# Attention and gated feed-forward in one kernel: a new order of the attention cycle, other cycles for the weight-narrowing jobs, all bias loads on one queue

## The chip, the cores and the metric

The kernel runs on one core of a Trainium2 chip. The metric is the device time of one execution in microseconds (us). Engines are named as in the profile: PE (TensorE, matrix products and transposes), DVE (VectorE), ACT (ScalarE), POOL (GpSimd) and SP (SyncE, which only issues DMAs here). L12 is line 12 of the kernel before.

## What is computed

Attention over 4 batches, 8 heads, 576 positions and head size 64, with a bias made from positions, and on its output a feed-forward block with a convolution of three taps and a gate, all in float32:

```python
scores = scale * np.matmul(q, k.transpose(0, 1, 3, 2))
...
bias = h @ w2
scores = scores + bias.transpose(2, 0, 1)[None, :, :, :]
...
attn = np.exp(scores)
attn = attn / (np.sum(attn, axis=-1, keepdims=True) + 1e-09)
return np.matmul(attn, v).astype(np.float32)
...
h = np.maximum(x @ w_in, 0.0)
...
gate = 1.0 / (1.0 + np.exp(-conv_out))
return (h * gate @ w_out).astype(np.float32)
```

## The kernel before, in words

The program has three stretches. First it makes the bias table (up to about 80 us). Then it works through 16 head pairs n = (p, b): pair p of heads, batch b, with b running fastest. Last comes the feed-forward block (from about 285 us), which keeps PE busy without a gap and which the change does not touch.

The attention stretch is a software pipeline, written out by hand as a list CYCLE (L888). Cycle m runs the entries for pair n = m and the first ones for pair m+1. An entry such as `S:3,1,0:P` has a name, a unit t (0 to 4, a block of query rows), a head h, an offset to m, and the engine. The program issues each engine's instructions in the order of the list, and an engine takes its instructions strictly in that order. The entries:

- S (scores, L438): products of queries and keys on PE into one of four pairs of PSUM banks. R (reduce, L471): DVE adds the bias tile and takes the row maximum. E (expo, L487): ACT exponentiates and sums rows.
- T and s (L531): PE transposes the exponentials. k0, k1, k0b, k1b and c copy them from PSUM to SBUF, on ACT or DVE by the letter at the end.
- P (L570): PE multiplies by the values, in groups 0 and 1 of five parts; xb copies the result out. P:0 is the last PE work of a cycle.
- ia, inv, sm, rt, st, sp: the row sums, inverted on DVE, turned on PE, copied, stored to DRAM and read back over all partitions into `rb`, of which there is one. AN (L638, L995): POOL multiplies the output of pair m-3 by rb.
- X (L229): for most pairs queries and keys are split for exact products into a high and a low part by POOL, in three pieces of two instructions each. `is_split(n)` is true for n = 3, 4, 6, 7, 8, 10, 11, 12 and 14, so X stands in cycles m = 2, 3, 5, 6, 7, 9, 10, 11 and 13. The first scores of pair m+1 need all three pieces.
- J1, J2, J3 and W (L875): the 28 jobs that narrow a piece of the feed-forward weights to float32 and split it. J1 is an integer shift on DVE (L161), J2 one ACT instruction, J3 an integer combination on DVE (L166), W two POOL instructions (L194, L195). J2 also issues the load for the third job after it. `per_pair` (L854) says how many jobs a cycle has; the unit of an entry (0, 2, 4) picks the first, second and third.

The three tiles that S, R, E and T of a unit share are used in turn, and a matrix product that takes a pair of banks waits for the copies or reductions out of it. Bias tiles for the next pair of heads are loaded in the cycles m = 3, 7 and 11 (b = 3), each as soon as its last reduction is issued; tiles 0 to 2 on SP's queue, 3 and 4 on POOL's (L248). `load(n + 2)` brings queries and keys after the last scores of pair n.

AN waits for the newest first shift of an earlier cycle:

```python
mul = apply_norm(n)
if shifts:
    tc.add_manual_dep(mul.ins, shifts.pop(max(shifts)).ins.name, DATA)
```

Of the kernel before, what the change touches and what calls it, by code (L numbers as in the profile page):

```python
# [13 lines left out]
ALU = mybir.AluOpType  # L14
# [4 lines left out]
def attention_ffn_kernel(  # L19
# [11 lines left out]
    nc = tc.nc  # L31
    B, S, DM = out.shape
# [5 lines left out]
    P = 128  # L38
# [159 lines left out]
    with tc.manual_schedule():  # L198
# [29 lines left out]

        def split_qk(n, k):  # L229
            x, lo, hi, cs = qks[n], qk_t[1][n % 2], his[(n + 1) % 2], chunks[k]  # L230
            nc.gpsimd.tensor_scalar(hi[:, cs], x[:, cs], 1.0, 0.0, op0=ALU.mult, op1=ALU.add)  # L231
            nc.gpsimd.tensor_sub(lo[:, cs], x[:, cs], hi[:, cs].bitcast(F32))  # L232

        vz_p = pool(att, "vz", 1)
# [11 lines left out]
            nc.sync.dma_start(vt[TL:P, 9], v[b, p, TL:P, 4])  # L246

        def load_bias(p, t, cuts=()):  # L248
            queue = nc.gpsimd if p and t not in (0, 1, 2) else nc.sync
            bt = bias_p.tile([P, 2, S], F32, name="bt") if t else bias0_p.tile([P, 1, S], F32, name="bt0")  # L250
            for a, e in zip((0,) + cuts, cuts + (P,)):
                for h in range(2):
                    c = (2 * p + h) * BW
                    if t:
                        i0 = TL + (t - 1) * P
                        queue.dma_start(bt[a:e, h], bias_rows[i0 + a:i0 + e, c:c + S])
                    else:
                        queue.dma_start(bt[TL * h:TL * h + TL, 0, :], bias_rows[0:TL, c:c + S])
            biast[p, t] = bt
# [21 lines left out]
        inv = bias_c.tile([P, 4 * NBLK], F32, name="inv")  # L281
# [114 lines left out]
        xb = {0: x0}  # L396
# [3 lines left out]
        DATA = mybir.DependencyInfo(mybir.DependencyClass.Sync, mybir.DependencyReason.DATA)  # L400
# [15 lines left out]
        def turned_sp(n, t):  # L416
            spt[n, t] = (sps[1][spt[n, t][1]], None)
# [317 lines left out]
        first = [(0, 0), (0, 1), (0, 2), (0, 3)]  # L735
# [4 lines left out]
        def heads(t):  # L740
            return (0, 1) if t else (0,)
# [109 lines left out]
                fill.extend(pv_parts(n, t > 2))  # L851

        NJ = 4 * KC + 2 * FE
        per_pair = [0, 0, 2, 2, 3, 2, 2, 1, 3, 2, 2, 1, 3, 2, 2, 1]  # L854
        first_job = {sum(per_pair[0:n]): n for n in range(NSEQ) if per_pair[n]}

        def job_slices(j):
            if j < 4 * KC:
                return w_in[j // 4 * P:j // 4 * P + P], wi[j // 4], slice(j % 4 * 256, j % 4 * 256 + 256)
            f = (j - 4 * KC) // 2  # L860
            return w_out[f * P:f * P + P], wo[f], slice(j % 2 * 256, j % 2 * 256 + 256)
# [8 lines left out]
        held = []  # L870
        now, used, drawn_at = [None], [0], [0]
        side_in = {}
        left, shifts = {}, {}

        def job_step(j, k):  # L875
            if k == 1:
                _, dst, cs = job_slices(j)
                jobs[j] = split_w_steps(e_p, dst[:, :, cs], raw_w.pop(j), ("cv", "cv"))
            ins = next(jobs[j])
            if k == 1 and j in first_job:  # L880
                shifts[first_job[j]] = ins
# [6 lines left out]
        CYCLE = """  # L888
            E:1,1,0:A X:0,1:G E:1,0,0:A S:2,0,0:P R:2,0,0:V S:2,1,0:P S:3,0,0:P X:1,1:G S:3,1,0:P ia:-1:A
            X:2,1:G R:2,1,0:V E:2,0,0:A s:1,0:P T:0,0:P k0:0,0:A P:1,0,-1:P R:3,1,0:V P:1,1,-1:P k1:0,0:A  # L890
            E:2,1,0:A P:1,2,-1:P R:3,0,0:V P:1,3,-1:P inv:-2:V E:3,1,0:A P:1,4,-1:P k1b:0,0:A k0b:0,0:V T:1,0:P
            AN:-3:G xb:1,-1:V inv:-1:V S:4,0,0:P S:4,1,0:P E:3,0,0:A J1:0,0:V k1:1,0:A s:2,0:P c:1,0:V k0:1,0:A
            T:2,0:P R:4,0,0:V R:4,1,0:V T:3,0:P J2:0,0:A S:0,0,1:P c:2,0:V k1:2,0:V E:4,0,0:A S:1,0,1:P k0:2,0:A
            J1:2,0:V E:4,1,0:A R:0,0,1:V S:1,1,1:P k1:3,0:A k0:3,0:V sm:-1:P J3:0,0:V s:4,0:P W:0,0:G J2:2,0:A
            sp:-2:G s:3,0:P T:4,0:P J3:2,0:V P:0,0,0:P P:0,1,0:P rt:-1:A R:1,1,1:V k1:4,0:V W:2,0:G J1:4,0:V
            J2:4,0:A J3:4,0:V W:4,0:G k0:4,0:A P:0,2,0:P R:1,0,1:V E:0,0,1:A P:0,3,0:P st:-1:G c:4,0:A P:0,4,0:P
            c:3,0:A xb:0,0:V
        """.split()

        begun = {(k, t, h, 2) for k, t, h in (  # L900
# [18 lines left out]
        def emit(op, copy):  # L919
            k, n = op[0], op[-1]  # L920
            t = op[1]
            if k == "S":
                scores(n, t, op[2])
                now[0] = pair[n, t, op[2]]
                used[0], drawn_at[0] = 0, len(clock)
                slots[now[0]][2] = -1 - len(clock)
                if (t, op[2]) == (4, 1) and n + 2 < NSEQ:
                    load(n + 2)
                    for later, x in held:
                        later(x)  # L930
                    held.clear()
            elif k == "R":
                reduce(n, t, op[2])
                left[n, t] = left.get((n, t), len(heads(t))) - 1
                p, b = seq[n]
                if not left[n, t] and b == B - 1 and p + 1 < NP:
                    load_bias(p + 1, t)
            elif k == "E":
                expo(n, t, op[2])
            elif k == "s":  # L940
                turned_sp(n, t) if spt[n, t][1] is not None else None
                side_of[n, t] = side_cols((n, t))
                side_transposes(side_of[n, t], n, t)
            elif k == "T":
                turned_sp(n, t) if spt[n, t][1] is not None else None
                turned[n, t] = transposes(n, t)
                after_turn(n, t)
            elif k in ("k0", "k1", "k0b", "k1b"):
                d, c = place(n, t, int(k[1]) if t else 0)
                v = turned[n, t][int(k[1])]  # L950
                done(turned_in[n, t])
                if t:
                    copy(d[:, 0:8, c:c + TL], v)
                elif k == "k0":
                    copy(d[:, 0:4, 0:TL], v[:, 0:4])
                elif k == "k0b":
                    copy(d[0:TL, 4, 0:TL], v[0:TL, 4])
                elif k == "k1":
                    copy(d[:, 5:9, 0:TL], v[:, 1:5])
                else:  # L960
                    copy(d[TL:P, 4, 0:TL], v[TL:P, 0])
            elif k == "c":
                d, c = place(n, t, 0)
                copy(halves(d[:, 8, c:c + P]), side_of.pop((n, t)))
                done(side_in.pop((n, t)))
            elif k == "P":
                g, c = op[1], op[2]
                if c == 0:
                    parts_of[n, g] = pv_parts(n, g, False)
                parts_of[n, g][c]()  # L970
                if (g, c) == (1, 4) and n + 2 < NSEQ:
                    if seq[n][1] == B - 1 and ("S", 4, 1, n + 1) not in begun:
                        held.append((load_v, n + 2))
                    else:
                        load_v(n + 2)
            elif k == "xb":
                pv_out(n, op[1], copy)
            elif k == "X":
                if is_split(n):
                    split_qk(n, t)  # L980
            elif k == "ia":
                add_eps(n)
            elif k == "inv":
                invert(n)
            elif k == "sm":
                sum_in[n] = side_cols(n)
                sum_transposes(sum_in[n], n)
            elif k == "rt":
                copy_sums(n, sum_in.pop(n), copy)
                done(side_in.pop(n))  # L990
# [38 lines left out]
        for m in range(1, NSEQ + 1):  # L1029
# [4 lines left out]
            for entry in CYCLE:  # L1034
                k, at, eng = entry.split(":")
# [117 lines left out]
        for b in range(B):  # L1153
# [28 lines left out]
            for c in range(KC):  # L1182
# [4 lines left out]
                lambda f, gi, t=t: gs[b, f][:, gi, t * P:(t + 1) * P] for t in range(NT)  # L1187
# [98 lines left out]
```

## Time and profile before

| | us |
|---|---|
| median of 3 runs (lowest to highest) | 481.1 (478.8 to 484.03) |
| the profiled execution | 480.15 |
| its span, first to last instruction | 478.3 |
| PE busy in the span | 458.1 |
| DVE, ACT, POOL busy | 350.9, 314.4, 162.9 |

The span is 1.85 us shorter than the execution's own time. The profile gives the busy time of each engine, what each waited for, and for any stretch a timeline. A PE that is shown busy can still have waited inside a group of instructions, so the length of a cycle, from one P:0 to the next, tells more than the idle time alone.

### The profile page before, as it was taken

What the parts mean: (1) busy time and instruction counts of PE and PEld (TensorE: products, weight loads), DVE (VectorE), ACT (ScalarE), POOL (GpSimd) and SP (SyncE); (2) the same over time, 40 slices, a digit from 0 to 9 for tenths busy, and PEclk for the clock granted to TensorE, in tenths of its full rate; (3) what the DMA queues carried; (4) which work ended last, traced back from release to release, by engine and by line L of the source; (5) the groups of instructions that cost most, each with busy time, mean ns of one, the idle gap of its engine ahead of it and who ended that gap; (6) DMA issues with size and microseconds to landing.
All of it is one profiled execution on the core that took longest, in us unless ns stands there. A gap on an engine that the chain in (4) does not pass through costs nothing.

```text
span 478.3 us, 10920 instructions
## 1 busy us (share of the span) xinstructions
PE 458.1 (96%) x4095; PEld 342.1 (72%) x4095; DVE 350.9 (73%) x818; ACT 314.4 (66%) x769; POOL 162.9 (34%) x194
## 2 busy tenths in 40 slices
PE   5988899999999999999999999999999999999996
PEld 3333356777677777777577768988888888888886
DVE  6999967788888788888888612893499149936971
ACT  6999876898888979988789722871364126414530
POOL 1000001493777837874667427006000500060000
PEclk9999999999999999999999999999999999999999
DMA  1899857688868977699861300001000200020003
GB/s 39 228 346 305 315 191 176 188 244 210 201 171 188 259 202 187 148 261 230 199 175 54 114 25 26 2 0 66 24 0 1 88 22 1 1 89 1 0 4 107
DMA packets 33768, 60.81 MB, mean 127 GB/s; under 512 B 6300, under 2 KB 15028, under 8 KB 33716
## 3 DMA queue, kind: packets, MB, share of 16 engines
q1 hardware_dynamic: 32372, 56.24, 41.8%
q0 software_dynamic: 960, 3.54, 2.8%
q8 instruction: 32, 0.52, 0.5%
q10 hardware_dynamic: 384, 0.35, 0.2%
q14 instruction: 20, 0.16, 0.1%
HBM read 44.12 MB, written 15.98 MB: 126 GB/s over the span
## 4 chain that ended last, share of the span: by engine, by line
PE 74%; DMA 11%; DVE 8%; issue 3%; ACT 2%; POOL 1%; SPq 0%; DVEq 0%
PE bank L108 35%; PE pair L108 31%; PE bank L111 7%; DMA bt<-bias_d 4%; DMA bias_d<-st 3%; DVE sp L476 2%; DVE y L325 2%; DVE ptx L155 1%; DMA vt<-in_v_dram 1%; ACT y L321 1%; DMA raw_w<-in_moe_w_in_dram 1%; ACT st L368 1%; DMA qk<-in_qk_dram 1%; DMA pars<-in_par_dram 1%; DVE pty L155 1%
## 5 line engine op out<-in xcount | busy, mean ns | idle before, releaser
L476 DVE CUSTOM_DVE_ANT_0 sp<-pair,bt 128x576 f32<-128x576 f32 x144 | 104.7, 751 | 17.8 <-PE pair L108 7.6
L490 ACT ACTIVATE sp<-sp,nm 128x576 f32<-128x576 f32 x144 | 111.2, 776 | 9.9 <-DVE nm L476 9.4
L108 PE MATMUL pair<-xs,wi 128*128 128x512 f32 x384 | 88.9, 391 | 0.0
L108 PE MATMUL bank<-wo,g 128*128 128x512 f32 x384 | 87.7, 389 | 0.0
L108 PEld LDWEIGHTS pair<-xs,wi 128*128 128x128 f32 x384 | 71.7, 188 | 15.7 <-issue 0.9
L108 PEld LDWEIGHTS bank<-wo,g 128*128 128x128 f32 x384 | 72.0, 188 | 14.9
L111 PE MATMUL bank<-identr,sr 64*128 64x64 f32 x1184 | 60.5, 245 | 5.1 <-DVE nm L476 3.0
L111 PEld LDWEIGHTS bank<-identr,sr 64*128 64x128 f32 x1184 | 53.8, 136 | 14.6 <-issue 5.8
L1071 DVE SCALAR_TENSOR_TENSOR cv<-h,cw,cv 128x575 f32<-128x575 f32 x64 | 52.3, 818 | 12.6 <-ACT cv L1066 10.6
L690 ACT ACTIVATE h<-pair 128x512 f32<-128x512 f32 x32 | 19.1, 597 | 55.5 <-PE pair L108 54.4
L231 POOL TENSOR_SCALAR hi<-qk 128x640 fp32r<-128x640 f32 (+1 forms) x27 | 19.2, 711 | 83.6 <-DMA qk<-in_qk_dram 79.4
L325 DVE TENSOR_SCALAR y<-tl,inv,nb 128x576 f32<-128x576 f32 (+33 forms) x112 | 47.6, 501 | 0.0
L194 POOL TENSOR_SCALAR xs<-x 128x512 fp32r<-128x512 f32 (+1 forms) x16 | 11.3, 704 | 105.4 <-DVE gt L1091 105.3
L108 PE MATMUL bank<-ptx,vt 128*64 128x320 f32 x320 | 47.0, 438 | 0.0
L108 PE MATMUL pair<-qk 64*128 64x288 f32 (+1 forms) x280 | 40.6, 433 | 4.0 <-DVE nm L476 2.7
L108 PE MATMUL pair<-y,pars 128*32 128x512 f32 (+8 forms) x352 | 42.3, 499 | 1.8 <-DVE y L325 1.0
L232 POOL TENSOR_TENSOR ql<-qk,hi 128x640 fp32r<-128x640 f32 (+1 forms) x27 | 41.0, 1517 | 2.3
L152 ACT ACTIVATE ptx<-bank 128x256 f32<-128x256 f32 (+2 forms) x92 | 39.1, 460 | 1.5 <-PE bank L111 0.8
L108 PE MATMUL bank<-pty,vt 128*64 128x256 f32 x320 | 38.1, 384 | 0.0
L1077 ACT ACTIVATE cv<-cv 128x576 f32<-128x576 f32 x32 | 21.9, 683 | 22.0 <-DVE cv L1071 21.9
L1078 DVE SCALAR_TENSOR_TENSOR cv<-cv,h 128x576 f32<-128x576 f32 x32 | 24.1, 752 | 14.0 <-ACT cv L1077 14.0
L108 PEld LDWEIGHTS pair<-y,pars 128*32 128x32 f32 x352 | 15.1, 112 | 26.4 <-DVE y L325 11.8
(90 smaller groups left out, 702.0 us busy)
## 6 DMA issues: line engine op xcount, KB each, us to landing
qk<-in_qk_dram SPq DMA_DIRECT2D x32, 320.0 KB
bias_d<-st SPq DMA_DIRECT2D x13, 607.0 KB
bt<-bias_d SPq DMA_DIRECT2D x18, 288.0 KB
qk<-in_qk_dram SPq DMA_DIRECT2D x32, 144.0 KB
rb<-r_d SPq DMA_DIRECT2D x32, 144.0 KB
vt<-in_v_dram SPq DMA_DIRECT2D x16, 256.0 KB
raw_w<-in_moe_w_in_dram SPq DMA_DIRECT2D x16, 256.0 KB
out_dram<-o SPq DMA_DIRECT2D x16, 256.0 KB
```

Source lines behind the costliest of these rows:

```text
L108: return use(nc.tensor.matmul(o, *args, **kw), o)
L111: return use(nc.tensor.transpose(o, *args), o)
L152: return noted(nc.scalar.activation(o, i, AF.Copy), i)
L231: nc.gpsimd.tensor_scalar(hi[:, cs], x[:, cs], 1.0, 0.0, op0=ALU.mult, op1=ALU.add)
L232: nc.gpsimd.tensor_sub(lo[:, cs], x[:, cs], hi[:, cs].bitcast(F32))
L325: nc.vector.tensor_scalar(y, dist[:, 0:n], inv[:, ig:ig + 1], nb1, op0=ALU.mult, op1=ALU.max)
L476: use(nc.vector.tensor_tensor_reduce(out=halves(spt[n, t][0][:, h]), in0=ps[:, :, 0:HS], in1=halves(bt[:, h]), op0=ALU.add, op1=ALU.min, s ...
L490: exps[n, t, h] = nc.scalar.activation(sp[:, h], sp[:, h], AF.Exp, bias=nm[:, h:h + 1], scale=-1.0, accum_out=sms[n][:, col:col + 1],)
L690: use(nc.scalar.activation(h[:, 0:NM], ps[:, 0], AF.Relu), ps)
L1071: nc.vector.scalar_tensor_tensor(out=cv[:, o:o + S - 1], in0=h[:, i:i + S - 1], scalar=cw[:, f, kk:kk + 1], in1=cv[:, o:o + S - 1], op0=AL ...
L1077: nc.scalar.activation(cv, cv, AF.Tanh, scale=0.5)
L1078: nc.vector.scalar_tensor_tensor(out=cv, in0=cv, scalar=1.0, in1=h, op0=ALU.add, op1=ALU.mult)
```

## The change

Six edits: the third piece of X waits for the newest J1 issued so far; AN waits for the newest J1 issued so far, and no longer for the newest first one; all bias tiles go to SP's queue; `per_pair` is new, with three jobs only in cycles without X and none or one where bias tiles are loaded; a cycle with fewer than three jobs leaves out the first places, not the last; and CYCLE is in a new order (its first line stands here).

```diff
-            nc.gpsimd.tensor_scalar(hi[:, cs], x[:, cs], 1.0, 0.0, op0=ALU.mult, op1=ALU.add)
+            first = nc.gpsimd.tensor_scalar(hi[:, cs], x[:, cs], 1.0, 0.0, op0=ALU.mult, op1=ALU.add)
+            if k == 2 and shifts:
+                tc.add_manual_dep(first.ins, shifts[-1].ins.name, DATA)
...
-            queue = nc.gpsimd if p and t not in (0, 1, 2) else nc.sync
+            queue = nc.gpsimd if p and t not in (0, 1, 2, 3, 4) else nc.sync
...
-        per_pair = [0, 0, 2, 2, 3, 2, 2, 1, 3, 2, 2, 1, 3, 2, 2, 1]
+        per_pair = [0, 0, 2, 1, 3, 2, 2, 0, 3, 2, 2, 0, 3, 2, 3, 3]
...
-        left, shifts = {}, {}
+        left, shifts = {}, []
...
-            if k == 1 and j in first_job:
-                shifts[first_job[j]] = ins
+            if k == 1:
+                shifts.append(ins)
...
-            E:1,1,0:A X:0,1:G E:1,0,0:A S:2,0,0:P R:2,0,0:V S:2,1,0:P S:3,0,0:P X:1,1:G S:3,1,0:P ia:-1:A
+            S:2,0,0:P E:1,0,0:A ia:-1:A inv:-1:V E:1,1,0:A T:0,0:P S:2,1,0:P S:3,0,0:P R:2,0,0:V J1:0,0:V
...
-                    tc.add_manual_dep(mul.ins, shifts.pop(max(shifts)).ins.name, DATA)
+                    tc.add_manual_dep(mul.ins, shifts[-1].ins.name, DATA)
...
-                if t // 2 < per_pair[n]:
-                    job_step(sum(per_pair[2:n]) + t // 2, 4 if k == "W" else int(k[1]))
+                job = t // 2 - (3 - per_pair[n])
+                if job >= 0:
+                    job_step(sum(per_pair[2:n]) + job, 4 if k == "W" else int(k[1]))
```

The instructions themselves stay as they are; lines after L232 move down by two or three. Three places in the order of the instructions follow.

PE in cycle 5, from the P:0 of cycle 4 on (ptx, vt), before: S of units 2 and 3 (qk), the side transposes of unit 1 and T of unit 0 (sr), P:1 (pty, vt), T of unit 1, S of unit 4, and so on.

```order
L108 MATMUL bank<-ptx,vt_112 64x320 x10
L108 MATMUL pair<-qk_56 128x288 x8
L111 MATMUL pair<-identr,sr_64 128x64 x2
L111 MATMUL bank<-identr,sr_63 128x64 x10
L108 MATMUL bank<-pty,vt_112 64x256 x10
L111 MATMUL bank<-identr,sr_64 128x64 x16
L108 MATMUL pair<-qk_56 128x288 x4
L111 MATMUL pair<-identr,sr_62 128x64 x2
```

The same place after:

```order
L108 MATMUL bank<-ptx,vt_112 64x320 x10
L108 MATMUL pair<-qk_56 128x288 x2
L111 MATMUL bank<-identr,sr_63 128x64 x10
L108 MATMUL pair<-qk_56 128x288 x8
L111 MATMUL bank<-identr,sr_64 128x64 x16
L111 MATMUL pair<-ident,rr_154 128x64 x2
L108 MATMUL pair<-qk_56 128x288 x2
L111 MATMUL pair<-identr,sr_64 128x64 x2
L111 MATMUL pair<-identr,sr_62 128x64 x2
L111 MATMUL bank<-identr,sr_62 128x64 x16
L108 MATMUL bank<-pty,vt_112 64x256 x10
L111 MATMUL bank<-identr,sr_63 128x64 x16
```

P:1 has moved behind S of unit 4 and T of units 1 and 2, and the scores of one pair now stand in three runs (2, 8 and 2 products) where there were two (8 and 4).

DVE in cycle 6 before (two jobs), with J1 (L161, into wu), R (L476, into sp), copies of transposes (into ptx, pty) and J3 (L166); the row with x_864 is the xb of P:1, and rows that only repeat are left out:

```order
L155 COPY x_864<-bank 128x256 [waits PE_49]
L623 RECIPROCAL rr_155<-rr_155 128x9
L161 TENSOR_SCALAR wu<-raw_w 128x256 [waits DMAHW3_49,DVE_49,Pool_49]
L155 COPY ptx<-pair 128x128
L476 ISA sp_60,nm<-pair,bt 128x576 [waits DVE_49,PE_49]
L155 COPY ptx<-bank 128x8x64 [waits PE_49]
L161 TENSOR_SCALAR wu<-raw_w 128x256 [waits DMAHW5_49,Pool_49]
L476 ISA sp_61,nm<-pair,bt_1123 128x576 [waits PE_49,Activation_49]
L155 COPY pty<-bank 128x8x64 [waits Activation_49]
L166 SCALAR_TENSOR_TENSOR wu<-wu 128x256 [waits DVE_49,Activation_49] x2
```

DVE in cycle 6 after, from the last R of unit 4 on:

```order
L478 ISA sp_60,nm<-pair,bt 128x576
L161 TENSOR_SCALAR wu<-raw_w 128x256 [waits DMAHW6_49,Pool_49]
L155 COPY x_864<-bank 128x256 [waits PE_49]
L155 COPY ptx<-bank 128x8x64
L155 COPY pty<-bank 128x8x64 [waits DVE_49,PE_49,Activation_49]
L478 ISA sp_61,nm<-pair,bt_1128 128x576 [waits PE_49,Activation_49]
L161 TENSOR_SCALAR wu<-raw_w 128x256 [waits DMAHW0_49,Pool_49]
L166 SCALAR_TENSOR_TENSOR wu<-wu 128x256 [waits DVE_49,Activation_49]
```

The first J1 now stands right in front of the xb of P:1, and the second one behind the first R of the next pair.

POOL in cycle 3 before: the last piece of X (hi, ql), the loads of bias tiles 3 and 4 (bt), AN (L641) between them, the first W, again without rows that repeat:

```order
L231 TENSOR_SCALAR hi_692<-qk_55 128x640 [waits Pool_49]
L232 TENSOR_TENSOR ql_57<-qk_55,hi_692 128x640 [waits Pool_49]
L256 DMA bt<-bias_d 128x576 [waits DVE_49]
L641 TENSOR_TENSOR x_127<-x_127,rb 128x576 [waits Activation_49]
L256 DMA bt<-bias_d 128x576 [waits DVE_49]
L194 TENSOR_SCALAR wi_693<-wu 128x256 [waits DVE_49]
```

POOL from the last piece of X in cycle 3 to the AN of cycle 4 (x_864) after:

```order
L231 TENSOR_SCALAR hi_692<-qk_55 128x640 [waits Pool_49]
L234 TENSOR_TENSOR ql_57<-qk_55,hi_692 128x640 [waits Pool_49]
L643 TENSOR_TENSOR x_127<-x_127,rb 128x576 [waits DMAHW6_49,Activation_49]
L194 TENSOR_SCALAR wi_693<-wu 128x256 [waits DVE_49]
L195 TENSOR_TENSOR wi_693<-wu,wi_693 128x256 [waits Pool_49]
L643 TENSOR_TENSOR x_864<-x_864,rb 128x576 [waits DMAHW7_49,DMAHW6_49,DVE_49]
```

The bias loads have left POOL; the AN of cycle 4 now waits for DVE, and the last piece of X has the same wait as before, on POOL alone.

## Rows read from the trace of the kernel before

**Rows 1.** Page, part 1: busy time of each engine.
```profile
PE 458.1 (96%) x4095; PEld 342.1 (72%) x4095; DVE 350.9 (73%) x818; ACT 314.4 (66%) x769; POOL 162.9 (34%) x194
```

**Rows 2.** Sums by stretch, each from P:0 to P:0.
```profile
core 0: us, PE busy (x) PEld busy (x) DVE busy (x) ACT busy (x) POOL busy (x), PEclk, DMA share, GB/s
95.23:259.49 164.26, 160.08 (x2142) 122.27 (x2140) 140.50 (x376) 142.68 (x385) 110.16 (x126) 1.00 0.78 199
95.23:109.37 14.14, 13.10 (x186) 10.45 (x184) 12.31 (x32) 11.87 (x32) 12.72 (x15) 1.00 0.92 243
109.37:122.43 13.06, 13.06 (x179) 9.80 (x177) 11.02 (x33) 11.88 (x32) 3.77 (x5) 1.00 0.81 204
...
150.61:163.70 13.09, 13.09 (x187) 10.45 (x185) 10.96 (x31) 11.69 (x31) 12.01 (x14) 1.00 0.96 253
...
217.64:231.91 14.27, 13.34 (x179) 9.80 (x177) 11.01 (x31) 12.16 (x32) 3.94 (x6) 1.00 0.93 227
```

**Rows 3.** Timeline, 105 to 110.6 us: start, length, engine, line, what, [idle before, releaser].
```profile
106.12 1.75 DVE L161 TENSOR_SCALAR wu<-raw_w 128x256 int32<-128x256 int32 x1
...
106.27 1.44 POOL L641 TENSOR_TENSOR x<-x,rb 128x576 f32<-128x576 f32 x1
...
107.80 0.74 DVE L476 CUSTOM_DVE_ANT_0 sp<-pair,bt 128x576 f32<-128x576 f32 x1
...
108.47 0.68 DVE L155 COPY pty<-bank 128x512 f32<-128x512 f32 x1
...
108.60 0.84 PE L111 MATMUL bank<-identr,sr 64*128 64x64 f32 x16 [1.04 <-DVE nm L476]
```

**Rows 4.** Line L161: duration in ns, least, median, most, and first and last start.
```profile
L161 DVE TENSOR_SCALAR wu<-raw_w x28: 231/401/1749, 90.5 to 267.8; 128x256 int32<-128x256 int32 x28
```

**Rows 5.** Groups of instructions, 95 to 260 us: busy us, mean ns | idle before.
```profile
L232 POOL TENSOR_TENSOR ql<-qk,hi 128x640 fp32r<-128x640 f32 x16 | 25.0, 1564 | 1.3
...
L161 DVE TENSOR_SCALAR wu<-raw_w 128x256 int32<-128x256 int32 x25 | 15.7, 629 | 0.0
...
L166 DVE SCALAR_TENSOR_TENSOR wu<-wu 128x256 int32<-128x256 int32 x27 | 12.1, 479 | 0.3
```

**Rows 6.** Waits, 95 to 260 us: us in total, times, longest.
```profile
PE bank L111 <- DVE nm L476: 3.0, 5, 1.0
...
DVE sp L476 <- DMA bt<-bias_d: 1.5, 1, 1.5
```

**Rows 7.** Timeline, 226 to 232 us.
```profile
228.65 0.76 DVE L476 CUSTOM_DVE_ANT_0 sp<-pair,bt 128x576 f32<-128x576 f32 x1 [1.50 <-DMA bt<-bias_d]
...
229.67 1.44 PE L108 MATMUL pair<-qk 64*128 64x288 f32 x8 [0.93 <-DVE ptx L155]
```

**Rows 8.** Timeline of PE, 95 to 104 us.
```profile
95.23 2.91 PE L108 MATMUL bank<-ptx,vt 128*64 128x320 f32 x20
98.07 0.40 PE L108 MATMUL pair<-hi 64*128 64x288 f32 x2
98.31 0.29 PE L108 MATMUL pair<-ql,hi 64*128 64x288 f32 x2
98.44 0.29 PE L108 MATMUL pair<-hi,ql 64*128 64x288 f32 x2
...
100.28 2.38 PE L108 MATMUL bank<-pty,vt 128*64 128x256 f32 x20
102.59 0.84 PE L111 MATMUL bank<-identr,sr 64*128 64x64 f32 x16
103.26 0.40 PE L108 MATMUL pair<-hi 64*128 64x288 f32 x2
```

**Rows 9.** Timeline of POOL, 95 to 106 us.
```profile
95.43 0.51 POOL L194 TENSOR_SCALAR wi<-wu 128x256 fp32r<-128x256 f32 x1 [6.70 <-DVE wu L166]
...
97.91 0.68 POOL L231 TENSOR_SCALAR hi<-qk 128x576 fp32r<-128x576 f32 x1
...
105.00 1.26 POOL L256 DMA_DIRECT2D bt<-bias_d  x2
```

More of the change, by code (lines that the diff above doesn't have):

```diff
@@ L888, in attention_ffn_kernel @@
         CYCLE = """
-            E:1,1,0:A X:0,1:G E:1,0,0:A S:2,0,0:P R:2,0,0:V S:2,1,0:P S:3,0,0:P X:1,1:G S:3,1,0:P ia:-1:A
[L890 to L897, printed above, removed]
+            S:2,0,0:P E:1,0,0:A ia:-1:A inv:-1:V E:1,1,0:A T:0,0:P S:2,1,0:P S:3,0,0:P R:2,0,0:V J1:0,0:V
+            k1:0,0:A S:3,1,0:P k0b:0,0:A k0:0,0:A k1b:0,0:A R:2,1,0:V S:4,0,0:P T:1,0:P X:0,1:G X:1,1:G sm:-1:P
+            E:2,0,0:A X:2,1:G E:2,1,0:A R:3,0,0:V R:3,1,0:V S:4,1,0:P k0:1,0:V k1:1,0:A s:1,0:P s:2,0:P
+            R:4,1,0:V c:2,0:V rt:-1:V E:3,1,0:A E:4,1,0:A T:2,0:P E:3,0,0:A P:1,0,-1:P P:1,1,-1:P P:1,2,-1:P
+            R:4,0,0:V c:1,0:A P:1,3,-1:P AN:-3:G P:1,4,-1:P J2:0,0:A J1:2,0:V k0:2,0:A E:4,0,0:A xb:1,-1:V
+            J3:0,0:V k1:2,0:V T:3,0:P S:0,0,1:P k1:3,0:A k0:3,0:V J2:2,0:A W:0,0:G sp:-2:G S:1,0,1:P R:0,0,1:V
+            J1:4,0:V S:1,1,1:P J3:2,0:V s:3,0:P s:4,0:P R:1,0,1:V c:3,0:A c:4,0:V E:0,0,1:A J2:4,0:A T:4,0:P
+            k1:4,0:A W:2,0:G st:-1:G P:0,0,0:P P:0,1,0:P P:0,2,0:P J3:4,0:V W:4,0:G P:0,3,0:P R:1,1,1:V
+            P:0,4,0:P k0:4,0:V xb:0,0:V
         """.split()
```

## The prediction

> **What bounds the kernel now.** I read part 1 of the page first: PE is busy for 458.1 of 478.3 us [rows 1]. So the first question is how long a cycle of the attention is, not how busy DVE or ACT are. The second view was the sums by stretch, from one P:0 to the next [rows 2]. The granted clock is 1.00 in every row, the full 2.4 GHz, so no difference between cycles is the clock's. The best cycles take 13.06 and 13.09 us, and there PE is busy for all of it; that is the floor of this PE work, 13.1 us. Others with the same products take 14.14 and 14.27. The twelve cycles from 95.23 to 259.49 take 164.26 us, against 12 x 13.1 = 157.2 at the floor: 7.1 us lie above it, in the whole stretch that the change touches. That bounds what any new order can win.
>
> Then the timeline of a bad cycle, to see who is late [rows 3]. POOL starts AN at 106.27 and ends it at 107.71. DVE starts J1 at 106.12, and it takes 1.75 us, to 107.87, 0.16 after AN has ended. The R behind it starts only at 107.80, its maximum is there at 108.47, and PE's transposes, which wait until that R frees a buffer, start at 108.60 after 1.04 us idle. A J1 takes 0.23 us at best and 1.75 at worst [rows 4], and the 25 of this stretch take 15.7 us, so 15.7 - 25 x 0.23 = 9.9 us of DVE time are such waits [rows 5]. PE waited five times for an R, 3.0 us in all [rows 6]. The other visible stall is a bias tile: an R waits 1.50 us for it, and PE 0.93 behind it [rows 7]. The rest of the 7.1 us is time in which PE counts as busy.
>
> The Trainium skill (SBUF — State Buffer, Who interferes with whom) says that VectorE and GpSimd share one pair of ports as an exclusive lock: a `tensor_scalar` that uses both ports waits until GpSimd's instruction ends, and so does a VectorE instruction with two SBUF inputs. The trace agrees on the first (J1 ends 0.16 us after AN). By the second J3 is exposed too; the trace has 479 ns for it on average. Were each of the 27 J3 to lose what a J1 loses on average, 0.4 us, DVE would need 10.8 us more by that rule; where that would decide is the second rival below.
>
> **The change part by part.** The wait of X's third piece. The order of POOL shows the same wait for that piece as before: the newest J1 belongs to an earlier cycle, and a W behind that J1 has already gone ahead on POOL, which implies the wait. Where a cycle has three jobs, and so a J1 ahead of X, there is no X. Cost and gain: 0.
>
> The wait of AN. It has force only in cycles with three jobs (4, 8, 12, 14, 15), where J1 stands behind the first R, about 1.4 us into the cycle; POOL has no X there. Queued behind AN is only a W, which waits for a later J3. Cost 0; at worst AN comes 1.4 us later than it could, and nobody waits for its result within the cycle.
>
> The new order. I lay out a cycle with the durations of the rows, P:0's end being 0. T of 16 transposes takes 103.26 - 102.59 = 0.67 us, T:0 with 10 takes 0.42, P:1 2.31, P:0 2.84 [rows 8]. The scores of one head are three steps of 0.13, so 0.40, and each run of scores begins with a step of 0.24, so 0.11 more [rows 8]. Then PE has: S2 0.5, T:0 to 0.9, four S to 2.6, T:1 to 3.3, S4 to 3.8, sides and T:2 to 4.6, P:1 to 6.9, T:3 to 7.6, three S of the next pair to 9.3, T:4 to 10.2, P:0 to 13.1. Against it DVE, with 0.67 for an R and 0.6 for a copy of 512 columns [rows 3]: the R of units 2 and 3 end at 1.3, 2.0, 2.7 and 3.3, those of unit 4 at 4.6 and 5.7. No PE step stands earlier than what it needs: T:3 at 6.9 wants the bank of an R that ended at 5.7, P:0 at 10.2 the bank of one that ends at 9.3.
>
> The first J1 would run at 5.7. POOL may then be in X's last piece, so it can be held by up to one such instruction, 1.56 us [rows 5]; but the next instruction on DVE is the xb, which waits for P:1 until 6.9 anyway. 1.2 of the 1.56 us are hidden there. If that cover is gone, everything behind xb is late by what is left. The second J1, at 9.3, finds POOL idle, since W waits for J3 and X is over.
>
> So the collisions should stop costing PE time. The gain is between 0 (all return elsewhere) and 7.1 us (all go); I take all but a residue. The best cycles before hold 0 to 0.1 us above the floor, and I put the residue at 0.07 a cycle, 0.8 us in twelve.
>
> What the order adds: the scores now stand in four runs per cycle for three. One more run start, 0.11 us x 12 = 1.3 us on PE, which has no cover. Bounds: 0 (a start that hides behind the transposes ahead of it) and 0.24 x 12 = 2.9 (the whole first step); 0.11 is what the rows show.
>
> The jobs. Cycles 3, 7 and 11 lose 1 job each (2, 1, 1 become 1, 0, 0), which lie in the stretches where the DMA engines are 0.92 and 0.96 busy [rows 2]; the last three cycles get them. There are 28 either way. The last weights are split later than before, but only the feed-forward's second product needs them, after the first one. 0.
>
> The bias tiles. Tiles 3 and 4 leave POOL, where each pair of issues takes 1.26 us and stands behind X (7.09 us from 97.91 to 105.00) [rows 9]. SP issues them as soon as their R is done, and their R in the next cycle comes 11 to 13 us later. That is the 1.17 us of the stretch from 217.64 (14.27 - 13.1), already in the 7.1. Behind them on SP stand the loads of values, the row sums and the next weights; late by some 2 us of issue at most, they have a cycle to land.
>
> The cycles outside the twelve (the first, and the last with the feed-forward's first products) I leave unchanged.
>
> **The sum.** -7.1 + 0.8 + 1.3 = -5.0 us, from the profiled execution's own 480.15 to 475.15. The median before is 0.95 higher (481.1); I go up by a third of that and forecast 475.5 us. A measurement of this kernel tells about 1% from no change, 4.8 us; the forecast lies right beyond that.
>
> **The rivals.**
>
> (1) The collisions move, they do not go. For it: J1 at 5.7 us still meets POOL, which works for 8.4 us on end in X and AN; AN hangs on rb, so its place varies. If J1 comes behind AN rather than behind X, it ends at about 8.1, 1.2 late for xb; R of the next pair and P:0's bank are late by what slack does not take, some 0.3 to 0.5 us per cycle. Against it: the cover by P:1. Twelve cycles x 0.35 = 4.2 us back: about 479.3, no change that could be told.
>
> (2) Slower: X becomes a loop of its own. The last J3 at about 11.1 releases W (1.24 us, half of the 2.48 from 95.43 to 97.91 [rows 9]), W releases X (7.09), and the scores of the next pair wait for X; from them the chain goes on over R (0.67), J1, J3, R, a copy and J3 (about 2.2 in all). With the scores' 0.9 that is 12.1 us, and some 0.1 us at each of three changes of engine makes 12.4, against 13.2 for PE. So 0.8 us of slack. It decides beyond 13.2, and costs 1 us per us in the nine cycles with X. Were J1 in it held by POOL as long as its worst one (1.5 us [rows 4]) and both J3 for the 0.4 us that a J1 loses on average (9.9 / 25), it would take 14.7: 9 x 1.5 = 13.5 us, 475.5 + 13.5 = 489.0. From a loop of 14.3 us on (9 x 1.1 = 9.9) the kernel is slower than before by 1%. Against it: at these J1 and J3 POOL has, by the layout, only W.
>
> (3) All 7.1 us go and the run starts hide: 480.15 - 7.1 = 473.0. For it: the transposes are a different kind of weight load; against it: the step after transposes at 103.26 looks like the one after P:0 (both 0.40) [rows 8].
>
> **How the numbers follow.** Forecast 0.55, rival 1 0.25, rival 2 0.11, rival 3 0.09. The forecast's own range, with run starts from 0 to 2.9 and the residue, is 473.4 to 477.1, so a little over half of it is faster by over 1%, the rest within 1%. With rival 3 faster gets 0.46, with rival 1 same gets 0.43, slower 0.11. The range from 472.5 to 481.5 takes in rival 3, rival 1 and the spread of the runs, and leaves out most of rival 2.
>
> **What would show it.** In the profile after: twelve cycles of about 13.2 to 13.3 us with no PE idle over 0.3; J1 longer than 0.5 us only right ahead of xb; four runs of scores with a first step of 0.24; no R waiting for a bias tile. The forecast is wrong if PE idles ahead of the first scores of the next pair for POOL (rival 2), or if J1's time is unchanged in sum and the R behind it is late (rival 1).

## The result and the profile after

The changed kernel takes 476.44 us in the median of 8 runs (475.48 to 477.8); the kernel before, on the same chip, takes 480.16. The ratio is 0.9917, with a 95% interval from 0.9887 to 0.9946: 3.7 us or 0.8% faster, inside the range and 0.9 us above the forecast. The profiled execution took 477.8 us, the longest of the eight. Here and below medians are of all runs, while ratios are of means and leave out runs more than 1.5% above the fastest of their kernel: two of the run with the old job places, one of the run with bias tiles on POOL's queue and single runs of the kernel before.

Page, part 1, of the changed kernel:

```profile
PE 457.5 (96%) x4095; PEld 342.4 (72%) x4095; DVE 361.2 (76%) x833; ACT 308.2 (65%) x754; POOL 156.1 (33%) x182
```

Against [rows 1] DVE has 10 us more, ACT 6 us and POOL 7 us less. PE, which sets the end, has 0.6 us less (458.1 to 457.5): of the 2.3 us that the span is shorter, the larger part is idle time of PE. Since a PE that is shown busy can hide waits, the cycles tell more.

Sums by stretch of the changed kernel, from P:0 to P:0 as in [rows 2]: cycles 3, 5, 7, 8, 12 and 14, and all twelve together (the stretch, its length, busy time and count of instructions of each engine, the granted clock, the share of the DMA engines):

```profile
core 0: us, PE busy (x) PEld busy (x) DVE busy (x) ACT busy (x) POOL busy (x), PEclk, DMA share, GB/s
95.05:108.07 13.02, 13.02 (x187) 10.45 (x186) 11.60 (x31) 11.06 (x31) 10.32 (x11) 1.00 0.95 269
...
121.20:134.67 13.47, 13.47 (x176) 10.16 (x174) 12.48 (x33) 11.46 (x32) 10.35 (x11) 1.00 0.72 177
...
147.69:160.71 13.02, 13.02 (x188) 10.44 (x186) 11.59 (x30) 11.04 (x31) 10.31 (x11) 1.00 0.87 246
160.71:175.91 15.20, 13.46 (x180) 9.83 (x178) 11.92 (x33) 11.29 (x32) 2.60 (x3) 1.00 0.93 208
...
215.40:230.12 14.72, 13.47 (x180) 9.85 (x178) 11.94 (x33) 11.30 (x32) 2.69 (x3) 1.00 0.77 184
...
243.59:257.29 13.70, 13.39 (x180) 9.87 (x178) 12.82 (x35) 11.91 (x33) 10.05 (x13) 1.00 0.40 110
...
95.05:257.28 162.23, 158.93 (x2142) 122.11 (x2140) 147.08 (x383) 136.69 (x372) 101.73 (x112) 1.00 0.77 196
```

The twelve cycles take 162.23 us for 164.26. In nine of them PE is busy throughout, at three lengths: 13.00 to 13.02 us where both pairs of a cycle are split (3, 6, 7, 10, 11), 13.13 in cycle 4, whose next pair is not split, and 13.47 in cycles 5, 9 and 13, whose own pair is not. Three are longer: cycles 8 and 12, with 15.20 and 14.72, and cycle 14 with 13.70. Cycle 3, which took 14.14 us before for J1 against AN, takes 13.02.

The line of J1 and two groups of 95 to 260 us (as in [rows 4, 5]):

```profile
L161 DVE TENSOR_SCALAR wu<-raw_w x28: 275/290/1521, 90.8 to 269.8; 128x256 int32<-128x256 int32 x28
```

```profile
L161 DVE TENSOR_SCALAR wu<-raw_w 128x256 int32<-128x256 int32 x23 | 14.3, 623 | 0.0
L166 DVE SCALAR_TENSOR_TENSOR wu<-wu 128x256 int32<-128x256 int32 x25 | 13.5, 540 | 0.3 <-ACT wu L162 0.3
```

The median J1 falls from 401 to 290 ns, but the mean hardly moves (629 to 623): fewer J1 are long, and those that are long last until the POOL instruction beside them has ended, X's last piece or AN. The waits of the same stretch tell that this no longer costs PE time. Engine waiting, what it waited for, us in total, times, longest:

```profile
DVE sp L478 <- DMA bt<-bias_d: 3.3, 2, 1.9
PE bank L111 <- ACT sp L492: 2.9, 2, 1.7
...
PE bank L111 <- DVE nm L478: 0.3, 1, 0.3
```

PE's wait for an R, 3.0 us before [rows 6], is 0.3. In its place R waits 3.3 us for a bias tile (1.5 before), and PE's 2.9 us stand behind that. The places are the R of unit 4 in cycles 8 and 12. Timeline of DVE and of PE in cycle 8:

```profile
169.76 0.76 DVE L478 CUSTOM_DVE_ANT_0 sp<-pair,bt 128x576 f32<-128x576 f32 x1 [1.91 <-DMA bt<-bias_d]
```

```profile
168.16 2.38 PE L108 MATMUL bank<-pty,vt 128*64 128x256 f32 x20
172.24 0.84 PE L111 MATMUL bank<-identr,sr 64*128 64x64 f32 x16 [1.71 <-ACT sp L492]
```

R finds tile 4 missing at about 167.8 and starts 1.9 us later; the exponential of unit 4 starts as much later, and T, which PE had next after P:1, waits 1.71 us. SP's queue shows why the tile was late (start, length, line, what; x2 are the tile's two halves):

```profile
152.71 3.60 SPq L258 DMA_DIRECT2D bt<-bias_d  x6
156.40 0.53 SPq L214 DMA_DIRECT2D qk<-in_qk_dram  x1
156.99 0.67 SPq L215 DMA_DIRECT2D qk<-in_qk_dram  x1
157.71 0.71 SPq L214 DMA_DIRECT2D qk<-in_qk_dram  x1
158.46 0.63 SPq L215 DMA_DIRECT2D qk<-in_qk_dram  x1
159.19 1.02 SPq L258 DMA_DIRECT2D bt<-bias_d  x2
```

Tile 4 goes out last, behind the next queries and keys (four transfers), 8.6 us before its R is ready for it, into DMA engines that are 0.87 to 0.93 busy in these two cycles.

### The profile page after: what moved, and what is told of

Same layout as the page of the kernel before. It is cut to its first block, busy times and chain, and to the rows that moved or that the text cites. A ratio compares the mean times of both kernels' runs of the same rounds, so it can differ in the third digit from the quotient of the medians.

```text
span 476.0 us, 10933 instructions
## 1 busy us (share of the span) xinstructions
PE 457.5 (96%) x4095; PEld 342.4 (72%) x4095; DVE 361.2 (76%) x833; ACT 308.2 (65%) x754; POOL 156.1 (33%) x182
## 4 chain that ended last, share of the span: by engine, by line
PE 77%; DMA 12%; ACT 5%; DVE 4%; issue 2%; SPq 0%; DVEq 0%; ACTq 0%
PE pair L108 34%; PE bank L108 34%; PE bank L111 8%; DMA bt<-bias_d 8%; DMA bias_d<-st 2%; ACT st L370 1%; DVE y L327 1%; ACT y L323 1%; DVE sp L478 1%; ACT sp L492 1%; PE pair L111 1%; DMA qk<-in_qk_dram 1%; DMA pars<-in_par_dram 1%; ACT tl L370 1%; DVE ptx L155 0%
## 5 line engine op out<-in xcount | busy, mean ns | idle before, releaser
L111 PE MATMUL bank<-identr,sr 64*128 64x64 f32 x1184 | 63.3, 246 | 5.0 <-ACT sp L492 4.5
L111 PEld LDWEIGHTS bank<-identr,sr 64*128 64x128 f32 x1184 | 56.1, 136 | 14.5 <-ACT sp L492 6.1
L108 PE MATMUL pair<-qk 64*128 64x288 f32 (+1 forms) x280 | 41.7, 433 | 2.0 <-DVE nm L478 1.8
L152 ACT ACTIVATE ptx<-bank 128x256 f32<-128x256 f32 (+1 forms) x92 | 33.5, 398 | 12.3 <-PE bank L111 11.5
L643 POOL TENSOR_TENSOR x<-x,rb 128x576 f32<-128x576 f32 x16 | 23.2, 1452 | 34.3 <-DMA rb<-r_d 27.8
```

The lines of the kernel that those rows point to most:

```text
L108: return use(nc.tensor.matmul(o, *args, **kw), o)
L111: return use(nc.tensor.transpose(o, *args), o)
L152: return noted(nc.scalar.activation(o, i, AF.Copy), i)
L643: return nc.gpsimd.tensor_mul(xb[b][:, p], xb[b][:, p], rbs.pop(n))
```

## The experiments

All are timed beside the kernel before; its median there was 480.5 to 481.4 us.

**What the old order loses, one edit at a time.** First, the kernel before with only AN moved, behind the second J1 (and waiting for that one):

```diff
-            AN:-3:G xb:1,-1:V inv:-1:V ...
+            xb:1,-1:V inv:-1:V ...
-            J1:2,0:V E:4,1,0:A ...
+            J1:2,0:V AN:-3:G E:4,1,0:A ...
```

> The kernel before with one move: AN stands behind the second J1 (the one at unit 2) and waits for it; the old order, jobs and queues otherwise. Theory 'collision' (what costs is that J1 waits out AN, and R and PE behind it): no J1 above 0.8 us at that place, the PE idles of 1.04, 0.35, 0.81, 0.38 and 0.38 us (3.0 in all) go, and some hidden time with them: 480.2 falls by 2 to 4 us, to 476 to 478. Theory 'order' (the gain of the change lies in the new places of scores, transposes and products): 479.5 to 480.5.

Measured: 477.65 us, ratio 0.995 (0.9912 to 0.9987); the twelve cycles take 160.68 us for 164.26. AN against J1 was a real loss. Second, the kernel before with only the bias tiles moved:

```diff
-            queue = nc.gpsimd if p and t not in (0, 1, 2) else nc.sync
+            queue = nc.gpsimd if p and t not in (0, 1, 2, 3, 4) else nc.sync
```

> The kernel before with all bias tiles on SyncE's queue and nothing else. As predicted (tile 4 came late because POOL issued it behind X): the wait of 1.5 us of an R and the 0.93 us of PE go, 479 to 479.5. Rival 'the queue is no matter, the DMA engines are full there': the tile comes as late as before or later, 480 to 481.5.

Measured: 477.98 us, 0.9938 (0.9916 to 0.996), more than either side expected. No R waits for a tile, and cycle 3 falls from 14.14 to 13.10: with no bias issues (1.26 us, [rows 9]) ahead of it on POOL, AN starts earlier (105.36 us) and is all but over when J1 comes, which takes 0.40 us. So the two losses of the prediction have one root in part, POOL's bias issues.

Both together in the old order:

> The kernel before with AN moved behind the second J1 and all bias tiles on SyncE's queue; old jobs, old order otherwise, no wait in X. Each edit alone gave 0.995 and 0.994 of the time before. Theory (both take away the same thing, the J1 that runs into AN, and a late bias tile is worth little in the old order): together no more than one alone, 0.992 to 0.995, 476.5 to 478. Rival (two separate losses): they add up to 0.988 to 0.990, 474.5 to 475.5, which is all that the whole change wins and more.

Measured: 476.74 us, 0.9916 (0.9899 to 0.9934), the time of the whole change. The medians of both lie below each alone (0.995, 0.9938) and above the sum, 0.989, but the intervals overlap. The traces tell more: the twelve cycles fall by 3.58 us with AN alone, by 2.90 with the bias alone, and by 3.95 (164.26 to 160.31) with both, not by 6.48. So the two edits mostly take away the same loss. Of the 2.06 us between the traced executions of AN alone and of both, 1.42 lie in cycle 2 (21.22 and 19.80 us), where the first J1 waits 1.9 us for its weights in the one, while the other shows no such wait.

**What the other parts give.** The changed kernel with the old CYCLE:

> The changed kernel with the old CYCLE: the new job table, places, waits and queue stay. Theory 'collision': the J1 of unit 2 still meets AN, since AN still stands ahead of it in the old order: 479 to 481, J1 again up to 1.5 us. If the gain came from the table, the waits or the queue: 476 to 477.5.

Measured: 478.8 us, 0.9961 (0.9943 to 0.9978). With the bias edit alone at 477.98, the other parts without the new order gain nothing (twelve cycles of 162.43 us against 161.36). The changed kernel without the two waits:

```diff
-            if k == 2 and shifts:
-                tc.add_manual_dep(first.ins, shifts[-1].ins.name, DATA)
...
-                if shifts:
-                    tc.add_manual_dep(mul.ins, shifts[-1].ins.name, DATA)
```

> The changed kernel without its two waits on the newest shift (third piece of X, and AN), all else kept. Theory (both waits are already given by what POOL does before, except AN's in five cycles): the same time as the changed kernel, 476 to 477. Rival (AN's wait holds POOL back in cycles 4, 8 and 12 and so pushes AN into the second J1 there, or the third piece's wait keeps J1 clear of X in the others): the J1 of 1.5 us at 171.5 and 225.7 disappear, or new ones come; 1 us or more to either side, 474.5 to 475.5 or 478 to 479.

Measured: 476.38 us, 0.9912 (0.9889 to 0.9935), the time of the changed kernel. Both waits cost nothing, as the prediction had it.

The changed kernel with the old table of jobs and the old rule for their places:

```diff
-        per_pair = [0, 0, 2, 1, 3, 2, 2, 0, 3, 2, 2, 0, 3, 2, 3, 3]
+        per_pair = [0, 0, 2, 2, 3, 2, 2, 1, 3, 2, 2, 1, 3, 2, 2, 1]
...
-                job = t // 2 - (3 - per_pair[n])
-                if job >= 0:
+                job = t // 2
+                if job < per_pair[n]:
```

> The changed kernel with the old job table and the old places (a cycle with two jobs has them at units 0 and 2). Theory 'collision': J1 of unit 0 now runs about 1.4 us into the cycle, beside X on POOL, in eight or nine cycles, and takes up to 1.7 us; the R behind it and T:1 are late: 478 to 482, slower than the changed kernel by 2 to 6 us. If the places of the jobs do not matter: 476 to 477.

Measured: 485.54 us, 1.0074 (1.0048 to 1.01), worse than either theory. Timelines of DVE and PE in cycle 2 of this kernel, then sums by microsecond in cycle 3:

```profile
89.66 0.29 DVE L161 TENSOR_SCALAR wu<-raw_w 128x256 int32<-128x256 int32 x1 [3.93 <-DMA raw_w<-in_moe_w_in_dram]
```

```profile
90.68 1.21 PE L111 MATMUL bank<-identr,sr 64*128 64x64 f32 x16 [3.39 <-DVE nm L478]
```

```profile
109.00:110.00 1.00, 1.00 (x12) 0.72 (x12) 1.00 (x5) 0.65 (x3) 1.00 (x1) 0.67 1.06 394
110.00:111.00 1.00, 1.00 (x8) 0.50 (x6) 0.98 (x4) 1.00 (x3) 0.31 (x1) 0.50 0.94 256
...
112.00:113.00 1.00, 1.00 (x10) 0.51 (x6) 0.00 (x0) 1.00 (x3) 0.00 (x0) 0.62 0.97 273
```

The first place of a cycle puts a J1 in cycle 2 that runs ahead of its weights: DVE waits 3.93 us, PE 3.39. In cycle 3 the J1 of the first place, right behind an R, meets X (1.69 us), and PE idles 1.05 us, from 106.09 to 107.14. And with each idle the granted clock falls to 0.50, the 1.2 GHz level: from about 88.9 to 95.7 us, and from about 109.3 to 112.8. Cycle 2 takes 25.89 us against 20.37 in the changed kernel, cycle 3 16.00 against 13.02: 8.5 us, of 9.0 between the two profiled executions (486.79 and 477.8). The stalls and the lower clock together make these 8.5; how much is the clock's was not told apart. To tell places from table, the old table with the new places:

> The changed kernel with the old table of jobs per pair (2, 2, 3, 2, 2, 1, ...) but its own rule for their places, so the first place of a cycle stays empty where there are fewer than three. Theory (the 9 us that the run with old table and old places lost against the changed kernel were mostly one wait, 3.4 us in cycle 2, of the first J1 for its weights, which came only because the first place was used there; single jobs in cycles 7, 11 and 15 cost little): 476.5 to 478.5. Rival (more weight loads in cycles 3, 7 and 11, whose DMA engines are full, make the bias tiles later still): 479.5 to 483.

Measured: 477.76 us, 0.9941 (0.9915 to 0.9967), beside 476.88 for the changed kernel, timed with it; 0.9 us is less than these intervals can tell. The loss is the place, not the table.

**The late tile.** The changed kernel, unedited, once more:

> The changed kernel once more, unedited, beside the two others on one chip, to compare its tile waits and its spread of times. Theory (a late tile 4 depends on when transfers land, so its time varies from run to run): 475 to 478, with a spread of 2 us or more, against 0.8 us for the kernel with tile 4 ahead. Rival (the spread is the chip's): a spread as narrow as that one's.

Measured: 476.88 us, 0.992 (0.9892 to 0.9949), 12 runs from 474.16 to 479.24. The profiled one is the fastest. Its sums by stretch for cycles 4, 8 and 12 and the whole, and from its timelines the issue of tile 4 and its R:

```profile
108.11:121.23 13.12, 13.12 (x179) 9.84 (x177) 12.32 (x35) 11.61 (x33) 3.69 (x5) 1.00 0.91 225
...
160.73:173.86 13.13, 13.13 (x178) 9.84 (x177) 10.94 (x34) 11.29 (x32) 2.56 (x3) 1.00 0.92 221
...
213.38:226.51 13.13, 13.13 (x179) 9.88 (x178) 11.77 (x33) 11.29 (x32) 2.54 (x3) 1.00 0.87 218
...
95.09:253.67 158.58, 158.27 (x2143) 122.11 (x2141) 145.73 (x383) 136.39 (x372) 101.39 (x112) 1.00 0.78 201
```

```profile
159.19 1.01 SPq L258 DMA_DIRECT2D bt<-bias_d  x2
```

```profile
167.80 0.75 DVE L478 CUSTOM_DVE_ANT_0 sp<-pair,bt 128x576 f32<-128x576 f32 x1
```

This is the same program, its tile 4 issued at the same 159.19, its R ready at the same 167.80, and here the tile is there. Cycles 8 and 12 take 13.13 us each instead of 15.20 and 14.72: 3.66 us, and the two executions differ by 477.8 - 474.16 = 3.64 us. So the late tile is the whole difference between these two executions, and a matter of when a transfer lands. Not all of the spread is the tile's, as the last experiment below shows.

Is it the queue, or the place in it? The changed kernel with tiles 3 and 4 on POOL's queue again:

> The changed kernel with one edit undone: bias tiles 3 and 4 go out on POOL's queue again, tiles 0 to 2 stay on SyncE's. Theory (tile 4 is late in cycles 8 and 12 because on SyncE's queue it stands behind the next queries and keys): on POOL it stands behind X instead, 1.3 us per pair of issues, so the stall of 1.9 us there becomes shorter or goes, but POOL's AN and X come later by up to 2.6 us in cycles 4, 8 and 12: net -2 to +1 us against the changed kernel, 474.5 to 477.5. Rival (POOL's issues were the worse of the two, as the prediction had it with 1.17 us per such cycle): the stall stays and J1 runs into AN again: 478 to 480.

Measured: 479.83 us, 0.9969 (0.9938 to 1.0), 475.23 to 483.58. The rival's time, its stall and its J1: one of 1.46 us at 108.29, beside AN and ahead of an R; three tiles late, 4.8 us of waiting, and cycles 4, 8 and 12 take 16.24, 15.32 and 14.36. In cycle 4 the clock fell too:

```profile
108.97:125.21 16.24, 14.86 (x179) 10.71 (x177) 13.40 (x38) 12.03 (x33) 5.43 (x8) 0.89 0.98 242
```

Then SP's queue kept, with tile 4 ahead of the queries and keys in the cycles that load bias:

```diff
                 if (t, op[2]) == (4, 1) and n + 2 < NSEQ:
-                    load(n + 2)
-                    for later, x in held:
-                        later(x)
-                    held.clear()
+                    if seq[n][1] == B - 1:
+                        held.append((load, n + 2))
+                    else:
+                        load(n + 2)
...
                 if not left[n, t] and b == B - 1 and p + 1 < NP:
                     load_bias(p + 1, t)
+                if not left[n, t] and t == 4:
+                    for later, x in held:
+                        later(x)
+                    held.clear()
```

> The changed kernel with one order altered on SyncE's queue: in the cycles that load the next pair's bias (3, 7, 11), bias tile 4 is issued ahead of the load of the next queries and keys, not behind it. Theory (place in the queue decides): tile 4 lands some 3 us earlier, the waits of 1.91 and 1.4 us for it in cycles 8 and 12 and the PE idle behind them go, 1.7 + 1.2 us: 473 to 475.5. Rival (the DMA engines are full there in any order, or the queries and keys become the late transfer in its place): 476 to 478.

Measured: 474.59 us, 0.9872 (0.9853 to 0.9891), all four runs from 474.04 to 474.84. Its SP queue and two sums by stretch (cycles 4 and 8), then POOL and DVE in cycle 4:

```profile
154.29 3.94 SPq L258 DMA_DIRECT2D bt<-bias_d  x8
158.32 0.63 SPq L214 DMA_DIRECT2D qk<-in_qk_dram  x1
```

```profile
108.00:121.51 13.51, 13.39 (x180) 9.84 (x178) 11.88 (x34) 11.56 (x33) 3.68 (x5) 1.00 0.93 194
...
161.02:174.15 13.13, 13.13 (x180) 9.84 (x178) 10.34 (x31) 11.29 (x32) 2.09 (x3) 1.00 0.95 223
```

```profile
117.61 1.42 POOL L643 TENSOR_TENSOR x<-x,rb 128x576 f32<-128x576 f32 x1 [7.05 <-DMA rb<-r_d]
...
118.35 0.96 DVE L166 SCALAR_TENSOR_TENSOR wu<-wu 128x256 int32<-128x256 int32 x1
```

Tile 4 goes out with the other tiles (x8 for x6), no R waits for a tile in the whole stretch, and the DMA engines are as busy as before (0.95). So at the same load the place in the queue decides. What is left shows in two cycles. In cycle 4 a J3 beside AN takes 0.96 us against a median of 0.42, the copies behind it are late, and the cycle takes 0.4 us more. Cycle 9 is taken up below.

How much of this is the new order's own? The same edit on the old order with AN late and bias on SP:

> The old order with AN late, all bias on SyncE's queue, and bias tile 4 issued ahead of the next queries and keys. It tells what the new order is worth once no tile is late in either. Theory (the old order uses tile 4 about 2 us later in its cycle and hardly waits for it, so the queue's order is worth 0 to 1 us there; what is left is a floor of 13.07 and 13.82 us per cycle against 13.02 and 13.47, 1.5 us in twelve cycles): 475.5 to 476.7. Rival (the queue's order is worth as much here as in the new order, 1.9 us): 474.3 to 475.2, and the new order is worth nothing by itself.

Measured: 475.38 us, 0.988 (0.9842 to 0.9919), between the two ranges. That the tile's place is worth 1.4 us here too (476.74 to 475.38) is not shown: the intervals overlap, and this order waits for no tile in either trace. Its twelve cycles:

```profile
94.56:254.42 159.86, 159.59 (x2142) 122.16 (x2140) 133.95 (x376) 142.44 (x385) 103.61 (x114) 1.00 0.79 203
```

Cycle 10 (13.65 us) holds a stall of some 0.55; without it the twelve take 159.3 us, at 13.06 to 13.12 and, in cycles 5, 9 and 13, 13.82 to 13.84. The new order needs 158.0 (below): it is shorter by about 0.36 us in cycles 5, 9 and 13, where the unsplit scores take 2.53 us instead of 2.96 (why was not settled), by 0.08 where both pairs are split, and longer by 0.05 in cycles 4, 8, 12 and 14. That is its own part of the gain, about 1.3 us in twelve cycles; the times alone (0.988 and 0.9872) do not tell the two apart.

Last, that kernel in the new order with one job moved from cycle 14, where J1 meets POOL's narrowing of the feed-forward's input, to cycle 7:

```diff
-        per_pair = [0, 0, 2, 1, 3, 2, 2, 0, 3, 2, 2, 0, 3, 2, 3, 3]
+        per_pair = [0, 0, 2, 1, 3, 2, 2, 1, 3, 2, 2, 0, 3, 2, 2, 3]
```

> The kernel with tile 4 ahead of the queries and keys, and one job moved from cycle 14 (3 jobs, 13.68 us, J1 meets the narrowing of the feed-forward's input) to cycle 7 (none before). Theory (cycle 14 falls to about 13.2, cycle 7 has room for one job in the last place; no tile is late, so the times lie close together): 473.7 to 474.6, with a spread of at most 1.5 us. Rival (the job in cycle 7 brings another weight load among the bias tiles and makes one of them late in cycle 8): 475 to 477 with a spread of 2 us or more.

Measured: 473.94 us, 0.9834 (0.9799 to 0.987), 473.24 to 476.45; a spread above the 1.5 us expected. Its profiled execution is the longest, yet its twelve cycles are the shortest of all (cycle 14 and the whole):

```profile
242.82:255.95 13.13, 13.13 (x179) 9.83 (x177) 12.35 (x33) 11.36 (x32) 10.16 (x12) 1.00 0.43 106
97.96:255.95 157.99, 157.99 (x2143) 121.97 (x2141) 144.35 (x383) 136.27 (x372) 102.94 (x113) 1.00 0.81 202
```

PE is busy for every microsecond, so this is what the work of the twelve cycles needs: 158.0 us. What made that execution long lies ahead of this stretch (its cycle 3 starts at 97.96 for 95.05 us), in the bias table; why was not settled. The version beats the kernel before by 1.3 to 2%, and its interval lies below the changed kernel's (0.9892 to 0.9949).

## Why the prediction was right, and which of its terms were wrong

**The main term was right.** AN against J1 was the loss named, and its cost goes: 3.0 us of PE waits for R become 0.3, and moving AN alone in the old order gives 0.995. J1 still meets AN (in cycle 8 of the changed kernel it takes 1.52 us at 171.51), but now ahead of xb, and that cover is wider than reckoned. The prediction had 1.2 of 1.56 us hidden behind xb's wait; a J1 of 1.31 us at 143.45 in the changed kernel costs its cycle nothing (13.02), and neither does the longest one, in cycle 9 of the kernel with tile 4 first:

```profile
183.80 1.66 DVE L161 TENSOR_SCALAR wu<-raw_w 128x256 int32<-128x256 int32 x1
174.15:188.04 13.89, 13.87 (x176) 10.20 (x174) 13.26 (x34) 11.57 (x32) 10.90 (x12) 1.00 0.81 196
DVE wu L161 <- POOL wi L195: 1.1, 1, 1.1
```

This cycle takes 0.42 us more than 13.47, but the time is lost before that J1: from P:0 to P:1 PE needs 8.35 us for the 7.93 of cycle 5 in the changed kernel's second trace (121.23 to 129.16), and from T:3 to the next P:0 it needs 3.22 in both. AN had waited for rb until 171.98, W stood behind AN, and a J1 at 174.62 waited 1.1 us for that W. So a late AN can cost time, though nobody waits for its result within the cycle, as the prediction had it: W waits behind AN, and J1 behind W.

Rival 1's sign, J1's time unchanged, came true (623 ns on average for 629), but not its harm. J1 over 0.5 us stood right ahead of xb, as forecast, but for one in cycle 14.

**"They have a cycle to land" was the wrong step.** It was the line on bias tiles 3 and 4: late by some 2 us of issue at most, cost 0. The new order asks for tile 4 8.6 us after its issue and not 11 to 13, and issues it last, behind four transfers, into engines 0.9 busy. So the sign "no R waiting for a bias tile" failed. It cost 3.7 us in the profiled execution and nothing in another of the same program; by the run with tile 4 first, 1.9 us in the median (476.44 to 474.59). The share of busy DMA engines stood in [rows 2], and the prediction used it for the weight loads but not for the tiles.

**The one floor was wrong.** It took 13.1 us for every cycle. What a cycle needs depends on which of its two pairs is split. In the new order it is 13.02 us in five cycles, 13.13 in the four whose next pair is not split (4, 8, 12, 14) and 13.47 in the three whose own pair is not (5, 9, 13; 13.8 in the old order with nothing stalled). The floor is 5 x 13.02 + 4 x 13.13 + 3 x 13.47 = 158.0 us for the 157.2 assumed, and the kernel of the last experiment reached it (157.99).

**The run starts cost nothing.** The prediction put 1.3 us on a fourth run of scores. Timeline of PE in cycle 8 of the changed kernel:

```profile
163.54 0.40 PE L108 MATMUL pair<-hi 64*128 64x288 f32 x2
163.78 0.29 PE L108 MATMUL pair<-ql,hi 64*128 64x288 f32 x2
163.91 0.29 PE L108 MATMUL pair<-hi,ql 64*128 64x288 f32 x2
164.04 0.51 PE L111 MATMUL bank<-identr,sr 64*128 64x64 f32 x10
164.38 0.40 PE L108 MATMUL pair<-hi 64*128 64x288 f32 x2
```

The first step of a run still takes 0.24 us (163.54 to 163.78), but T:0 behind it takes 0.34 (164.04 to 164.38), not the 0.42 reckoned. Cycles with both pairs split are 13.02 us long, 0.07 under the best before (13.09), and those whose next pair is not split 13.13, 0.07 above theirs (13.06). In sum the lower bound, 0, was nearest.

**The sum again.** In the execution without a late tile: -7.1, +0.8 for the floor, +0.6 of residue (predicted 0.8), nearly all of it in cycle 14, 0 for starts, makes -5.7; measured 158.58 - 164.26 = -5.7. Its time, 474.16, lies 6.0 below the profiled one before. The median is 2.3 to 2.7 us above that. So errors of both signs, starts too dear by 1.3, the floor too low by 0.8 and the tile too cheap by about 2, nearly cancelled. That is luck: the forecast of 475.5 was nearer than its terms.

**The rest.** Both waits void: shown. Jobs at no cost: shown for the table within what can be told; cycle 14 pays 0.55 us for its third job. Rival 2, the loop over X: no PE wait for POOL appears in the traces. By the Trainium skill (SBUF — State Buffer, Who interferes with whom) a VectorE instruction with two SBUF inputs contends with a GpSimd instruction that reads SBUF; the trace agrees, with the J3 of 0.96 us beside AN that ends 0.28 after it. On average J3 rose only from 479 to 540 ns.

## What to carry to other kernels

When a new order asks for a buffer earlier in its cycle, work out the time from issue to use for every transfer into it, and count what stands ahead of it on its queue; where the DMA engines are 0.9 busy, put first what is wanted first. A J1 that is slow beside POOL is no loss by itself: look at what stands behind it and whether that would have waited anyway. And profile a kernel with a spread of times more than once: here the difference between two executions of one program named the stall to the tenth of a microsecond.

## What was not expected of the hardware

**One program, one tile, two landings.** The same issue time gave a tile that was there after at most 8.6 us (167.80 - 159.19) in one execution and after some 10.5 in another, at a DMA share of 0.92 and 0.93 in that cycle. The two parted before the tile was issued. From 153 to 159 us, late execution first:

```profile
153.00:159.00 6.00, 6.00 (x98) 4.99 (x96) 4.93 (x14) 5.98 (x16) 5.75 (x5) 1.00 0.82 245
153.00:159.00 6.00, 6.00 (x98) 5.00 (x96) 4.94 (x14) 5.98 (x16) 5.75 (x5) 1.00 0.95 319
```

The late one moved 245 GB/s in these 6 us, the other 319. From 159 to 167.8 the engines were busy throughout in both (shares 1.04 and 1.02), so the late one did not catch up. Why it moved less is open. The Trainium skill (DMA: Bandwidth & Descriptors, Queues, rings and completion order) says that on each DMA engine the descriptors of one queue are taken in order; moving four transfers behind the tile, which took its waits away, agrees with that.

**A short idle can cost more than itself.** In the kernel without waits the same late tile in cycle 8 left PE idle for 1.70 us, as in the changed kernel (1.71), but the cycle took 16.42 us and not 15.20. The idle, and sums by microsecond behind it:

```profile
172.46 0.84 PE L111 MATMUL bank<-identr,sr 64*128 64x64 f32 x16 [1.70 <-ACT sp L490]
```

```profile
173.00:174.00 1.00, 1.00 (x16) 0.40 (x14) 1.00 (x3) 1.00 (x3) 0.36 (x1) 0.83 0.87 213
174.00:175.00 1.00, 1.00 (x8) 0.82 (x6) 1.00 (x3) 0.95 (x4) 0.78 (x2) 0.50 1.02 220
...
176.00:177.00 1.00, 1.00 (x18) 0.88 (x14) 0.58 (x1) 0.47 (x2) 0.87 (x2) 0.50 1.12 303
```

After the idle the granted clock falls from 1.00 to 0.50, the 1.2 GHz level, from about 173.7 until about 177; in the changed kernel's profiled execution it stayed at 1.00 after the same idle. Why one and not the other was not settled. In no trace without such a stall did the clock fall within the twelve cycles.
